# An attention and feed-forward kernel: batch 0 by halves of heads, first units by halves of features, weight columns dealt in pairs

## The chip, the core and the metric

The kernel runs on one core of a Trainium2 chip. The core has five engines with an instruction queue each: TensorE (PE) for matmuls, VectorE (DVE), ScalarE (ACT), GpSimd (POOL) and SyncE (SP), which here only issues DMAs. [...] Engines wait for one another on semaphores. The metric is the device time of one execution in microseconds, the median over runs.

## What is computed

Linear attention, then a feed-forward layer with a gated activation:

```python
q_s = softmax(q, over head_dim)            # q, k, v: 8 batches, 8 heads, 576 rows, 64
k_s = softmax(k, over the rows)
kv  = einsum('bhsd,bhse->bhde', k_s, v)
x   = einsum('bhsd,bhde->bhse', q_s, kv)   # -> 4608 tokens x 512 features
h   = x @ w_in                             # 512 -> 2048
g   = h / (1 + exp(-beta * h))
out = g @ w_out                            # 2048 -> 512
```

## The kernel before

**Tiles.** Every token of x is needed by both dense layers, so x, h and g never leave the chip. Tokens are cut into nine chunks of 512: for each batch the first 512 of its 576 rows (chunks 0 to 6 and 8), and one chunk, the eighth, of the 64 rows left over in each of the eight batches. A chunk passes through 16 units; unit u makes 128 of the 2048 features of h: four matmuls (`h`, over the four 128-wide k tiles of x, L889) into a PSUM bank, a tanh on ACT (`th`, L907), a multiply on DVE (`g`, L924; the sigmoid is written with tanh), and four matmuls with w_out (`o`, L959), one for each 128 tokens, that add into the four accumulators `acc`. After the 16 units the accumulators are copied to SBUF (`oev`) and stored (`st`). Four PSUM banks are a ring (`hT`) for everything else, the other four are `acc`.

**Attention of a batch.** Heads are held two to a tile: j = 0 to 3 counts pairs of heads, J = 0, 1 halves of the heads (J = 0 is j 0 and 1). For q: row maximum (`qmax`, DVE), subtract (`qsub`, POOL), `qexp` (ACT), `qsum` and `qrcp` (DVE), `qnorm` (POOL), transposes (`qtr`, PE, and `qtrev` on ACT or DVE). For k: a maximum over the rows by DVE (`kmax`, then `kred` over the nine row groups, then `kswap` and `ksmall`, which take the larger of partition halves), `krep` spreads it, `ksub` subtracts it (POOL or DVE), `kexp` (ACT). v is cast to bf16 (`vcast`). Then `kv` (72 small matmuls), `kvn` (five DVE instructions that divide by the sum), `x` (eight matmuls), and `xev`, four evictions to xT.

**Order.** All instructions are issued in one order written out by hand, ORDER: each engine runs its own in that order, and waits where an operand isn't there. All loads are issued by SP in that order too. `fill` operations are matmuls with zeros or leftover data that keep PE busy while it waits.

**Batch 0 before.** q's rows come in three parts, h = 0, 1 (four row groups each) and 2 (the ninth). For k the pairs j = 0, 1 are subtracted on PE: `kin` multiplies k by an fp32 identity, `kminus` adds the maximum times minus the identity in the same bank, and `kexp` reads PSUM. `x 0 h J` makes x for half of the tokens, h, from all heads; `h n h x` and `th n h`, `g n h`, `o n h` of units 0 to 3 then run on 256 tokens at a time, two units sharing a bank.

**Weights.** w_in is cut in four blocks of 512 columns, w_out in four of 512 rows, and each of the eight in two halves: 512 KB each, `ld w0` to `ld w7` into four staging buffers, then cast to bf16 (`cast w`). w_in's blocks are w0, w2, w4, w6 and serve units 0-3, 4-7, 8-11, 12-15; their halves are k tiles 0, 1 and 2, 3. w_out's are w1, w3, w5, w7.

**Tail.** For the last eight units the `o` operations are split by token tile, and token tile 3 also by output columns: columns 0-255 stay in acc[3], columns 256-511 go to a ring bank and are copied out by ACT and by DVE, 128 each.

Of the kernel before, what the change touches and what calls it, by code (L numbers as in the profile page):

```python
# [1069 lines left out]
```

## Time and profile before

| | us |
|---|---|
| median of 3 runs (lowest, highest) | 287.24 (287.19, 287.53) |
| the profiled execution | 287.31 |
| its span, first to last instruction | 285.5 |
| PE busy | 275.8 |
| DVE, ACT, POOL busy | 194.9, 174.2, 131.2 |
| DMA moved | 50.01 MB |

The page counts an engine as busy while an instruction of it is under way; matmuls overlap, so the distance between starts says what one costs. The chain of waits is followed back from the last instruction to what released each. In the timelines a row is start, duration, engine, line, operation, result and operands, count, and in brackets the idle time ahead of it with what ended it; rows of the chain are start, duration, what. Rows of groups end with busy time, mean ns of one, and idle time with its releasers. "PEld" is PE's load of a matmul's stationary operand.

### The profile page before, as it was taken

How to read it: one execution, taken by the hardware profiler on the slowest of the kernel's cores; microseconds unless marked ns; L12 is line 12 of the kernel's file. 1: busy time of each engine (PE TensorE's matmuls, PEld its weight loads, DVE VectorE, ACT ScalarE, POOL GpSimd, SP SyncE). 2: the span in 40 equal slices, each digit the busy share in tenths (PEclk: the TensorE clock that was granted, in tenths of full speed). 3: DMA queues.
4: the chain of work that ended last, by engine and by line, in shares of the span. 5: the costliest groups of instructions: out<-in, count | busy, mean ns of one | idle time of the engine just before them, and what ended most of it. 6: DMA issues, size and time to landing. Idle time of an engine off the chain costs nothing.

```text
span 285.5 us, 5163 instructions
## 1 busy us (share of the span) xinstructions
PE 275.8 (97%) x1947; PEld 129.9 (45%) x1977; DVE 194.9 (68%) x394; ACT 174.2 (61%) x291; POOL 131.2 (46%) x93
## 2 busy tenths in 40 slices
PE   7799999999999999999999999999999999999994
PEld 2356544444444544444444544444444444444442
DVE  2998957999899898997667858555754263435421
ACT  2498885887488577837586566564671274345422
POOL 6899996869379948083960650090020000000000
PEclk9999999999999999999999999999999999999999
DMA  7999999990991994991434927000054001005104
GB/s 229 390 391 385 384 389 391 390 336 7 276 371 43 316 275 181 295 329 41 152 119 113 189 62 193 0 3 2 0 141 164 0 0 39 0 0 187 73 0 147
DMA packets 37048, 50.01 MB, mean 175 GB/s; under 512 B 15760, under 2 KB 16160, under 8 KB 37024
## 3 DMA queue, kind: packets, MB, share of 16 engines
q1 hardware_dynamic: 36880, 49.63, 53.4%
q8 instruction: 15, 0.25, 0.3%
q10 hardware_dynamic: 144, 0.07, 0.1%
q14 instruction: 9, 0.07, 0.1%
HBM read 36.71 MB, written 9.44 MB: 162 GB/s over the span
## 4 chain that ended last, share of the span: by engine, by line
PE 91%; DMA 4%; ACT 1%; SPq 1%; issue 1%; DVE 0%
PE hT L889 43%; PE acc L959 42%; DMA kf<-in_k_dram 2%; DMA wst<-in_moe_w_in_dram 2%; PE hT L638 2%; PE hT L688 1%; SPq L275 1%; PE hT L951 1%; PE acc L951 1%; ACT w_in_b L232 0%; PE hT L464 0%; PE hT L734 0%; ACT qT L232 0%; ACT ek L612 0%; ACT ek L605 0%
## 5 line engine op out<-in xcount | busy, mean ns | idle before, releaser
L907 ACT ACTIVATE th<-hT,beta_c 128x512 bf16<-128x512 f32 (+1 forms) x148 | 96.6, 677 | 66.9 <-PE hT L889 48.5
L924 DVE SCALAR_TENSOR_TENSOR g<-th,hT 128x512 bf16<-128x512 bf16 x144 | 94.6, 680 | 58.5 <-ACT th L907 55.5
L959 PE MATMUL acc<-w_out_b,g 128*128 128x512 bf16 x543 | 130.7, 379 | 1.4 <-issue 0.8
L889 PE MATMUL hT<-xT,w_in_b 128*128 128x512 bf16 (+1 forms) x517 | 117.7, 372 | 0.7 <-issue 0.2
L889 PEld LDWEIGHTS <-w_in_b 128*128 128x128 bf16 x592 | 57.6, 98 | 64.8 <-ACT w_in_b L232 0.2
L959 PEld LDWEIGHTS <-g 128*128 128x128 bf16 x560 | 53.7, 98 | 64.5 <-issue 2.9
L560 POOL TENSOR_TENSOR kf<-kf,kmb 128x1152 f32<-128x1152 f32 (+1 forms) x15 | 38.0, 2543 | 23.6 <-DVE kmb L550 17.6
L441 POOL TENSOR_TENSOR qn<-eqe,qz 128x1152 bf16<-128x1152 bf16 (+2 forms) x20 | 34.5, 1739 | 28.0 <-DVE qz L433 18.1
L393 POOL TENSOR_TENSOR qf<-qf,qm 128x1152 f32<-128x1152 f32 (+2 forms) x20 | 34.4, 1733 | 18.4 <-issue 11.9
L378 DVE TENSOR_REDUCE qm<-qf 128x9 f32<-128x576 f32 (+2 forms) x34 | 23.3, 704 | 6.2 <-DMA qf<-in_q_dram 6.2
L422 ACT ACTIVATE eqe<-qf 128x576 bf16<-128x576 f32 (+2 forms) x34 | 21.5, 657 | 9.5 <-POOL qf L393 9.5
L232 ACT CAST xT<-hT 128x512 bf16<-128x512 f32 x19 | 12.6, 740 | 21.1 <-PE hT L688 21.1
L428 DVE TENSOR_REDUCE qs<-eqe 128x9 f32<-128x585 bf16 (+2 forms) x34 | 24.0, 713 | 0.5 <-ACT eqe L422 0.4
L490 DVE TRANSPOSE_TENSOR_REDUCE km<-kf 128x18 f32<-128x576 f32 x32 | 23.6, 754 | 0.0
L612 ACT ACTIVATE ek<-kf 128x576 bf16<-128x576 f32 x30 | 19.5, 683 | 0.9 <-DMA vf<-in_v_dram 0.9
L234 POOL CAST va<-vf 128x1152 bf16<-128x1152 f32 (+1 forms) x11 | 12.0, 1105 | 6.9 <-DMA vf<-in_v_dram 6.9
L889 PE MATMUL hT<-xTt,w_in_b 128*128 128x512 bf16 x63 | 14.9, 379 | 0.1
L234 DVE CAST xT<-hT 128x512 bf16<-128x512 f32 x9 | 6.3, 728 | 7.0 <-PE hT L688 7.0
L232 ACT COPY osb<-acc 128x512 f32<-128x512 f32 x14 | 7.8, 594 | 3.0 <-PE acc L959 3.0
L367 PE MATMUL hT<-g,warm 128*128 128x512 bf16 x21 | 7.0, 482 | 1.6 <-POOL g L240 1.5
L234 DVE COPY osb<-acc 128x512 f32<-128x512 f32 (+1 forms) x6 | 3.8, 632 | 4.9 <-PE acc L951 3.8
L638 PEld LDWEIGHTS <-ek 64*64 64x64 bf16 x576 | 5.7, 106 | 2.2 <-issue 1.3
(74 smaller groups left out, 121.7 us busy)
## 6 DMA issues: line engine op xcount, KB each, us to landing
qf<-in_q_dram SPq DMA_DIRECT2D x14, 576.0 KB, 6.9
kf<-in_k_dram SPq DMA_DIRECT2D x14, 576.0 KB, 7.7
vf<-in_v_dram SPq DMA_DIRECT2D x14, 576.0 KB, 8.4
out_dram<-osb SPq DMA_DIRECT2D x19, 256.0 KB, 2.6
wst<-in_moe_w_in_dram SPq DMA_DIRECT2D x8, 512.0 KB, 7.9
wst<-in_moe_w_out_dram SPq DMA_DIRECT2D x8, 512.0 KB, 11.2
out_dram<-wst SPq DMA_DIRECT2D x16, 256.0 KB, 3.7
qf<-in_q_dram SPq DMA_DIRECT2D x4, 288.0 KB, 4.1
```

The lines of the kernel that those rows point to most:

```text
L234: eng.tensor_copy(dst, src)
L378: dve.tensor_reduce(qm[:, j : j + n, i0:i1], qf[b % 2][:, j : j + n, i0:i1], axis=AX.X, op=ALU.max,)
L393: eng.tensor_tensor(x, x, m, ALU.subtract)
L422: act.activation(eq[:, i0:i1, j : j + n, :].rearrange("p i j d -> p j i d"), x, ACTF.Exp)
L428: dve.tensor_reduce(qs[:, i0:i1, j : j + n].unsqueeze(3), x, axis=AX.X, op=ALU.add)
L441: eng.tensor_tensor(qn[b % 2][:, i0:i1, j : j + n, :], eq[:, i0:i1, j : j + n, :], z, ALU.mult)
L490: dve.tensor_reduce(km[:, j : j + n].rearrange("p j i e -> p (j i e)"), kf[b % 2][:, j : j + n].rearrange("p j i (e c) -> p (j i e) c", c=32),
L560: eng.tensor_tensor(x, x, m, ALU.subtract)
L889: pe.matmul(w, w_in_b[:, kt, u * P : (u + 1) * P], r, start=(kt == 0), stop=(kt == KT - 1),)
L907: act.activation(th[turn(n, h) % 3][:, c], bank(n, h), ACTF.Tanh, scale=beta_c[:, u : u + 1])
L924: dve.scalar_tensor_tensor(out=out, in0=of, scalar=1.0, in1=src, op0=ALU.add, op1=ALU.mult)
L959: pe.matmul(acc[t][:], g[n % NG][:, t * P : (t + 1) * P], w_out_b[:, u, :], start=(u == 0), stop=(u == NJ - 1),)
```

## The change

Batch 0 goes by halves of heads all the way: `kred`, `kswap`, `ksmall`, `kvn` and `x` are done for J = 0 and J = 1 apart, with `krep` and `ksub` for each j (j even on DVE, j odd on POOL); nothing of k is subtracted on PE any more, and the constants for it go. Batch 1's k is treated the same way up to `ksub`. The first two thirds of q of J = 0 are not subtracted by POOL: ACT's exp takes minus the maximum as a bias, one instruction for each row group and j. Units 0 to 3 start with k tiles 0, 1 (the features of J = 0) on all 512 tokens and finish with k tiles 2, 3; units 2 and 3 take two accumulators as their banks (SPARE), so the first `o` waits for their gates.

Unit u makes the columns 256 (u // 2) + 2 c + u % 2 of w_in: two units share 256 neighbouring columns, one the even and one the odd, so the stationary operand of `h` has a step of two. w_out's rows are loaded two neighbouring rows to a partition, and beta is transposed in two strided parts. w_in_b is laid out as block, half, pair of units, and then 512 columns and 64 unused.

The last token tile is cut at column 384 in place of 256: 384 columns in acc[3], 128 in a ring bank, one copy each. ORDER is written anew throughout.

The start of ORDER:

```diff
-ld_q0_0, ld_q0_1, ld_q0_3, consts, qmax_0_2_0, qmax_0_0_0, qmax_0_1_0, qsub_0_2_0=pool, qsub_0_0_0=pool, qexp_0_0_0,
-ld_q0_2, fill_0, ld_k0_3, qmax_0_0_1, ld_k0_1, fill_8, ld_k0_0, qmax_0_1_1, qmax_0_2_1, ld_k0_2, qsub_0_0_1=pool,
...
+consts, ld_q0_1, ld_q0_0, qmax_0_0_j1, qmax_0_0_j0, qmax_0_1_j1, qmax_0_2_0, qexp_0_0_j1, ld_q0_3, qexp_0_0_j0,
+ld_q0_2, qsub_0_2_0=pool, qmax_0_1_j0, qsum_0_0_0, qrcp_0_0_0, qexp_0_2_0, qexp_0_1_j1, qexp_0_1_j0, ld_k0_1,
+qmax_0_1_1, qsub_0_1_1=pool, qmax_0_0_1, qsub_0_0_1=pool, ld_beta, ld_k0_0, ld_v0_0, ld_k0_3, ld_v0_1, kmax_0_1,
+kmax_0_0, qsum_0_1_0, ld_k0_2, ld_v0_2, fill_0, fill_5, fill_7, fill_10, fill_14, ld_v0_3, ld_w0_0, kred_0_0,
+qrcp_0_1_0, qexp_0_1_1, fill_12, fill_6, fill_1, qnorm_0_0_0=pool, fill_3, fill_13, fill_4, kswap_0_0, qtr_0_0_0,
+kmax_0_3, ksmall_0_0, krep_0_1, qexp_0_0_1, qsum_0_0_1, qnorm_0_1_0=pool, ld_w0_1, fill_8, qtrev_0_0_0=act, kmax_0_2,
+qtr_0_1_0, vcast_0_j0=act, fill_2, ksub_0_1=pool, qtrev_0_1_0=act, qrcp_0_0_1, krep_0_0, ld_w2_0, ld_w2_1, kred_0_1,
+ld_q1_1, vcast_0_j1=act, kswap_0_1, qnorm_0_0_1=pool, ksub_0_0=dve, kexp_0_1, ksmall_0_1, fill_11, beta_tr, krep_0_3,
+krep_0_2, kexp_0_0, qtr_0_0_1, ksub_0_3=pool, vcast_0_j3=act, cast_w0_0_1=act, qsum_0_1_1, ksub_0_2=dve, kexp_0_2,
+qrcp_0_1_1, kv_0_0, kexp_0_3, kvn_0_0, ld_w1_0, qmax_0_2_1, qtrev_0_0_1=dve, fill_9, x_0_0, xev_0_0=dve,
+vcast_0_j2=pool, kv_0_1, qnorm_0_1_1=pool, cast_w0_1_0=pool, kvn_0_1, qsub_0_2_1=pool, cast_w0_0_0=pool, qtr_0_1_1,
+xev_0_1=act, h_2_0, h_3_0, cast_w2_0=pool, qtrev_0_1_1=act, ld_w1_1, cast_w2_1=pool, x_0_1, xev_0_3=dve, ld_w4_0,
+cast_w0_1_1=act, qexp_0_2_1, qsum_0_2_0, qsum_0_2_1, qrcp_0_2, qnorm_0_2_1=pool, cast_w1_0=pool, h_0_0, h_1_0,
+ld_w4_1, xev_0_2=act, beta_ev, h_1_1, th_1, ld_q1_0, ld_w3_0, h_0_1, qmax_1_2, h_3_1, h_2_1, ld_k1_1, ld_w6_0,
+qmax_1_3, th_0, g_0, th_2, h_5, g_2, th_5, g_1, th_3, ld_w6_1, g_3, qsub_1_1=pool, h_6, h_4, h_7, th_4, g_5, th_6,
+g_4, g_6, ld_w3_1, cast_w1_1=pool, o_0, o_1, o_2, o_3, qnorm_0_2_0=pool, cast_w4_0=pool, qexp_1_2, qexp_1_3,
...
```

The code:

```diff
-    FILLS = [(14, None)] + [(2, (h, J)) for h in range(2) for J in range(2)] + 8 * [(1, None)]
-    KPE = range(2)
-    QPE = set()
+    FILLS = [(14, None)] + [(2, (h, J)) for h in range(2) for J in range(2)] + 10 * [(1, None)]
+    BIAS = {(0, 0), (1, 0)}
...
-    w_in_b = sbt("w_in_b", [P, KT, FF], BF16)
+    w_in_b = sbt("w_in_b", [P, NJ // 4, 2, 2, 4 * P + 64], BF16)
...
-    w_out_v = w_out.rearrange("(j p) f -> p j f", p=P)
+    w_out_v = w_out.rearrange("(m p r) f -> p m r f", p=P, r=2)
...
-            cast(eng, w_in_b[:, 2 * half : 2 * half + 2, 512 * blk + c0 : 512 * blk + c1], s)
+            m0, m1 = c0 // (2 * P), c1 // (2 * P)
+            dst = w_in_b[:, blk, half, m0:m1, 0 : 4 * P].rearrange("p m (k c) -> p m k c", c=2 * P)
+            cast(eng, dst, s.rearrange("p k (m c) -> p m k c", c=2 * P))
...
-                for c, (c0, c1) in enumerate(((0, P), (P, 512))):
+                for c, (c0, c1) in enumerate(((0, 2 * P), (2 * P, 512))):
...
+    def q_exp_rows(j, n, i0, i1):
+        uses("qmax", *q_parts(0, j, n, i0, i1))
+        made("qexp", *q_parts(0, j, n, i0, i1))
+        made("qsub", *q_parts(0, j, n, i0, i1))
+        for a in range(j, j + n):
+            for i in range(i0, i1):
+                act.activation(eq[:, i, a, :], qf[0][:, a, i, :], ACTF.Exp, bias=qm[:, a, i : i + 1])
...
+    def k_cut(J):
+        return slice(0, KT) if J is None else slice(2 * J, 2 * J + 2)
...
-    def k_swap(b):
-        uses("kred", b)
-        take(("swap", b))
-        made("kswap", b)
+    def k_swap(b, J):
+        uses("kred", *pairs_of(b, 2 * J, 2))
+        take(("swap", b, J))
+        made("kswap", (b, J))
         pe.matmul(
-            place[("swap", b)][:, 0 : 2 * KT],
+            place[("swap", b, J)][:, 0:4],
             swap[:],
-            kmr[:, :, :, 0].rearrange("p j e -> p (j e)"),
+            kmr[:, k_cut(J), :, 0].rearrange("p j e -> p (j e)"),
...
-    def kv_norm(b):
-        uses("kv", (b, 0), (b, 1))
+    def kv_norm(b, J=None):
+        Js = (0, 1) if J is None else (J,)
+        c = slice(Js[0], Js[-1] + 1)
+        uses("kv", *[(b, x) for x in Js])
...
-    def x_mm(b, J, h=None):
-        i0, i1 = (0, NM) if h is None else (4 * h, 4 * h + 4)
+    def x_mm(b, J):
         uses("kvn", (b, J))
...
+            for jp in range(2):
+                place[("x", b, 2 * J + jp)] = acc[2 * jp + J][:]
...
+    SPARE = {2: 0, 3: 2}
+
+    def bank(n):
+        if ("h", n) not in place:
+            if n in SPARE:
+                uses("xT", *[(0, jp) for jp in range(2)])
+                place[("h", n)] = acc[SPARE[n]][:]
+            else:
+                take(("h", n))
+        return place[("h", n)]
...
             pe.matmul(
                 w,
-                w_in_b[:, kt, u * P : (u + 1) * P],
-                r,
+                w_in_b[:, u // 4, kt // 2, u // 2 % 2, 2 * P * (kt % 2) + u % 2 : 2 * P * (kt % 2) + 2 * P : 2],
+                x[:, kt],
...
-    LAST_PIECES = ((0, 0, 256), (1, 0, 128), (1, 128, 128))
+    PIECES = ((0, 384), (384, 512))
...
+            for b in range(2):
+                to = pool if j % 2 else dve
+                op(f"krep {b} {j}", lambda b=b, j=j, to=to: k_rep(b, j, 1, to))
+                op(f"ksub {b} {j}", lambda e, b=b, j=j: k_sub(b, j, 1, e), "pool" if j % 2 else "dve")
...
-        if n < LEAD:
-            for h in range(2):
-                for x in range(2):
-                    op(f"h {n} {h} {x}", lambda n=n, h=h, x=x: st1(n, (x, x + 2), h))
-                op(f"th {n} {h}", lambda n=n, h=h: tanh(n, h))
-                if n % 2 == 0:
-                    op(f"g {n} {h}", lambda n=n, h=h: gate(n, h))
-                op(f"o {n} {h}", lambda n=n, h=h: st2(n, h))
-            continue
-        if n in (16, 17):
+        if n < LEAD or n in (16, 17):
             op(f"h {n} 0", lambda n=n: st1(n, (0, 1)))
             op(f"h {n} 1", lambda n=n: st1(n, (2, 3)))
```

The end of ORDER, after the last `o` operations of token tiles 0 to 2:

```diff
-o_141_3_0, o_142_3_0, o_143_3_0, st_8_1, oev_8_3_0=dve, oev_8_2=act, st_8_2, st_8_3_0, o_140_3_1, o_141_3_1,
-o_142_3_1, o_143_3_1, oev_8_3_1=act, oev_8_3_2=dve, st_8_3_1, st_8_3_2
+oev_8_3_0=act, oev_8_2=dve, st_8_2, o_136_3_1, o_137_3_1, o_138_3_1, o_139_3_1, o_140_3_1, o_141_3_1, st_8_1,
+st_8_3_0, o_142_3_1, o_143_3_1, oev_8_3_1=dve, st_8_3_1
```

The last store is issued on ACT's queue, the one of columns 0-383 on SP's.

More of the change, by code (lines that the diff above doesn't have):

```diff
@@ L359, in fill @@
         done.add(key)
[L360 removed]
+        r, w = g[NG - 1][:], place[key]
         if part is not None:
@@ L928 @@
[L928 to L937 removed]
+        v = NJ // 2 * (u % 2) + u // 2
+        uses("st1", n)
+        if n >= 3:
+            uses("gate", n - 3)
+        made("tanh", n)
+        act.activation(th[n % 3][:], place[("h", n)], ACTF.Tanh, scale=beta_c[:, v : v + 1])
```

523 lines of the change are left out of this document (188 added, 335 removed).

## The prediction

> **What bounds the kernel now.** I read the page first (busy shares, slices, chain), then the chain of waits in order of time, the timelines of TensorE (PE), VectorE (DVE), ScalarE (ACT) and GpSimd (POOL) over the first 40 us, and the groups with shapes kept apart. The page:
>
> ```profile
> PE 275.8 (97%) x1947; PEld 129.9 (45%) x1977; DVE 194.9 (68%) x394; ACT 174.2 (61%) x291; POOL 131.2 (46%) x93
> PE   7799999999999999999999999999999999999994
> PE 91%; DMA 4%; ACT 1%; SPq 1%; issue 1%; DVE 0%
> ```
>
> PE is the bound of every slice but the first two and the last. The chain in order of time (start, us, what) shows where that begins and ends:
>
> ```profile
> 4.03 6.47 DMA kf<-in_k_dram
> 10.52 5.99 DMA wst<-in_moe_w_in_dram
> 16.51 0.67 ACT ek L612
> ...
> 19.72 0.41 PE acc L688 x8
> ...
> 20.67 7.01 PE hT L889 x48
> ...
> 32.11 0.45 PE hT L464 x8
> ...
> 45.10 0.71 PE hT L638 x71
> ...
> 49.16 3.45 PE hT L889 x16
> ...
> 69.89 0.18 PE hT L734 x8
> ...
> 76.86 0.56 PE hT L688 x8
> ...
> 281.44 0.45 PE hT L951 x4
> 281.92 0.28 ACT osb L232
> 282.21 0.29 DVE osb L234
> ```
>
> Until 20.67 us the chain is loads, ACT and small matmuls; from there to 281.9 it is matmuls, 261.2 us. Sixteen of 512 columns take 3.45 us, 215.6 ns each, and the two dense layers are 1152 of them or as many columns: 248.4 us. The seven later batches add kv (0.71) and x (0.56) each, 8.9 us; transposes of batch 1 (0.45 twice) and the tails' eight small products (up to 0.18 each) make some 2. So 259 of the 261.2 us must be done by every version, and the end moves by three things only: when the stream of h matmuls starts, what is added to it or waits in it, and the tail behind it.
>
> **The start.** The twelve loads of batch 0 come in both versions at one pace, all of q before k and v; the new order puts w_in's first block right behind them, where the old one has half of q of batch 1 between. The first h matmuls of the change need features of heads 0 to 3 alone, so k and v of these. By my count DVE is latest there. Its timeline and groups:
>
> ```profile
> 7.63 1.48 DVE L378 TENSOR_REDUCE qm<-qf 128x8 f32<-128x512 f32 x3 [1.68 <-DMA qf<-in_q_dram]
> 9.71 1.26 DVE L428 TENSOR_REDUCE qs<-eqe 128x8 f32<-128x520 bf16 x2
> 11.71 1.39 DVE L490 TRANSPOSE_TENSOR_REDUCE km<-kf 128x18 f32<-128x576 f32 x2
> 18.24 0.23 DVE L657 TENSOR_SCALAR kz<-hT 128x2 f32<-128x2 f32 x2
> 18.72 0.49 DVE L660 TENSOR_TENSOR kvn<-hT,kz 128x128 bf16<-128x128 f32 x2
> ...
> L560 DVE TENSOR_TENSOR kf<-kf,hT 128x576 f32<-128x576 f32 x1 | 0.7, 715 | 0.0
> L433 DVE RECIPROCAL qz<-qs 128x8 f32<-128x8 f32 x4 | 0.5, 168 | 0.0
> L234 DVE CAST xT<-acc 128x512 bf16<-128x512 f32 x2 | 1.4, 740 | 0.2 <-ACT beta_c L349 0.2
> ```
>
> The last of q lands at 7.63. From there the new order gives DVE, ahead of the first kvn: 2 qmax of 128x512 (0.60 apart: 1.2), 4 kmax (half of 1.39: 2.8), 3 qsum (half of 1.26: 1.9), 2 ksub (j 0 and 2 are DVE's now; 0.70: 1.4) and 11 small ones (2 kred, 3 qrcp, 2 ksmall, 4 krep) at some 0.15, near the 168 ns row: 1.65. Sum 8.95: DVE reaches kvn at 16.6. The whole kvn took 18.24 to 19.21, 0.97; half of it is as many instructions on half the columns, I take 0.75: 17.35. x of half 0 on PE is 0.56: 17.9. Its two evictions run side by side on DVE and ACT, 0.74: 18.65, and with the hand-overs **h_2 starts at 18.8**.
>
> The others are not later. Rows of POOL and ACT, groups and timeline:
>
> ```profile
> L393 POOL TENSOR_TENSOR qf<-qf,qm 128x512 f32<-128x512 f32 x4 | 4.1, 1046 | 2.1 <-DVE qm L378 2.1
> L441 POOL TENSOR_TENSOR qn<-eqe,qz 128x512 bf16<-128x512 bf16 x4 | 4.1, 1046 | 0.3
> L560 POOL TENSOR_TENSOR kf<-kf,kmb 128x576 f32<-128x576 f32 x1 | 1.4, 1411 | 0.1
> L422 ACT ACTIVATE eqe<-qf 128x128 bf16<-128x128 f32 x2 | 0.5, 302 | 1.7 <-POOL qf L393 1.7
> ...
> 6.51 0.63 ACT L422 ACTIVATE eqe<-qf 128x512 bf16<-128x512 f32 x1 [4.28 <-POOL qf L393]
> ```
>
> From 8.3 (first qmax of q's second half) POOL has 2 subs and 4 norms of 1.02, 2 ksub of 1.4, a vcast of some 0.65: 9.6, so 17.9, where the last norm is wanted for x of half 1. The sixteen ACT exps with a bias (128x64, an unseen form) take the place of two POOL subs and two large exps. Each costs between nothing and the 302 ns of a 128x128; I take 0.2 for half its columns: 3.2 us, at most 4.8. They need no sub, so they start at about 5, where ACT's first exp now starts at 6.51, and end by 9.8 at the latest, before POOL is through with subtracting q's second half (8.3 + 2 x 1.02 = 10.3). Cost nothing; without that cover it would be the excess over 10.3.
>
> PE then does h_2 and h_3 on two of four k tiles (4 x 0.216), x of half 1 (0.56), h_0 and h_1 while x of half 1 is evicted (0.86 over 0.74), then the other halves: no gap from 18.8. But x of half 1 stands in this stream, and in the old one ahead of it, so 18.8 + 0.56 = 19.4 compares with 20.67: **-1.3 us**. Bounds: 0 if each of DVE's 22 steps costs 0.06 more than I took; -1.9 if the small ones pack 0.1 apart.
>
> **What is added to the stream.** Two kswap of batch 1, fp32, and the strided columns of w_in. Rows of PE's weight loads, and where a cast was late:
>
> ```profile
> 13.42 0.30 PEld L507 LDWEIGHTS hT<-kmr,swap 128*128 128x128 f32 x2
> L889 PEld LDWEIGHTS <-w_in_b 128*128 128x128 bf16 x592 | 57.6, 98 | 64.8 <-ACT w_in_b L232 0.2 <-issue 0.2
> L580 PEld LDWEIGHTS acc<-kf,ident_f 128*128 128x128 f32 x4 | 0.7, 188 | 1.3 <-issue 1.2
> 34.88 1.04 POOL L234 CAST w_in_b<-wst 128x1024 bf16<-128x1024 f32 x1
> 36.38 1.05 ACT L232 CAST w_in_b<-wst 128x1024 bf16<-128x1024 f32 x1
> 37.48 1.08 PEld L889 LDWEIGHTS <-w_in_b 128*128 128x128 bf16 x6 [0.22 <-ACT w_in_b L232]
> ```
>
> A kswap is two passes with two fp32 loads, 0.11 apart: 0.22 each, **+0.4 us**; 0 if loads are pulled under the matmuls ahead, +0.8 if the 0.39 us that the pair spans is exposed.
>
> Strided columns: a load of 128 bf16 two apart covers the 512 bytes per partition that an fp32 load covers, and that one took 188 ns, 0.11 apart. The plain one takes 98 ns and lies under a matmul of 216, so nothing is paid up to there: **0**, and at most 0.1 for each time that PE starts after a wait, some ten times: +1. It is below zero for no reason.
>
> The weights of units 12 on: in the old run PE arrives as ACT's cast ends and loses 0.22. Now PE comes 1.3 earlier. POOL, counted on from the two w_in casts behind its last norm, does qsub 2.1, norms and casts of 1.04 one after another, waits for q's sums of batch 1 until about 29.3 and ends cast_w6_0 at 35.5, 0.4 before the 35.92 of now; ACT's cast behind an exp that waits for POOL ends at some 36.2, PE is there at 35.6 and does half a unit on the first half (0.43): **+0.3 us**; 0 to 1.2 (ACT's cast as late as now).
>
> k of batch 1 by halves puts two ksub (1.4) and two qtrev on DVE. Its waits between 36 and 48 us:
>
> ```profile
> DVE g L924 <- ACT th L907: 3.3, 2, 2.3
> ```
>
> The 3.3 us that it waits for tanh there take them; without that cover they delay gates and come out of the 1.3. The paired rows of w_out halve the number of its packets; the loads of weights are all landed long before PE asks but for those above. Nothing for either.
>
> **The tail.** Before, the last 256 columns are evicted by ACT, then DVE (0.28 and 0.29 in a row, though meant side by side). Now one DVE copy of 128 columns is behind the last matmul: **-0.3 us**; 0 if the 384 columns' store, started 0.5 earlier and three times as large, lands last.
>
> **Sum.** -1.3 + 0.4 + 0.3 - 0.3 = -0.9. The profiled execution took 287.31 us (span 285.5 and 1.8 around it), 0.07 over the median of the runs, 287.24: 287.31 - 0.9 = **286.4 us**.
>
> **The rivals.** (a) *PE's clock falls in the thinner start, slower.* The old start keeps PE busy by fp32 matmuls with the identity, which go away; the fills that stay are ten of 0.22 between 8 and 18.8. The trace shows a slow PE at the very start (windows: sum over 8 to 20 us, then two stretches of the first fills; between them a row of PE's timeline):
>
> ```profile
> sum 12.00, PE 9.96 PEld 5.10 DVE 11.49 ACT 8.72 POOL 11.29; mean PE 1.66 PEld 0.85 DVE 1.91 ACT 1.45 POOL 1.88
> 13.05 0.40 PE L464 MATMUL acc<-ident,qn 128*128 128x128 bf16 x4 [1.08 <-POOL qn L441]
> 1.40:4.90 3.50, 3.45 (x9) 1.00 0.89 254
> 4.90:6.90 2.00, 2.00 (x9) 1.00 0.92 324
> ```
>
> Nine fills take 3.5 us from 1.4 us on and 2.0 after that. From 8 to 20 us PE is now busy 9.96 of 12; of the new 10.8 us I find some 5: 2.2 of fills, 1 of transposes, 1.5 of kv and x. If that lets the slow state return, and it holds as long as at the start, the first 3.5 us of h run 9 where 16 fit: 1.5 us lost, 287.9. It decides once a gap is longer than those that the old run bears, 1.08 us at most; the new one, from the last early fill to the first exp of q's second half, is 8.3 to 10.1 by my count. [...]
>
> (b) *The gain is given back.* POOL, ACT and DVE are near full until 36 us; if ACT's casts are no earlier than now, PE waits 1.2 instead of 0.3 at unit 12: 287.3. For it speaks the 0.22 wait, against it that POOL is rid of two subs of 1.02.
>
> (c) *Waits in the stream go too.* 261.2 less 259 leaves 2.2 us lost inside it; a cast that writes one piece of w_in_b is less tied to matmuls that read its neighbours. Half of it: 285.3. Against it: only 0.2 of PEld's idle time ends on a w_in cast.
>
> (d) *The change of columns does not stay hidden.* If a strided load took four times 98 ns, 392, each of 576 h matmuls would be 176 ns longer: 388. Against it the 188 ns row. [...]
>
> **How the numbers follow.** The forecast 0.46, with 285.7 to 287.1 as its own range; (a) 0.16, (b) 0.16, (c) 0.17, (d) 0.05. The measurement tells 0.2% (0.57 us) from no change. Faster by that is under 286.67: three quarters of the forecast, all of (c), a little of (b): 0.54. Within: the rest of the forecast, most of (b), a little of (a): 0.22. Slower: most of (a), (d), a little of (b): 0.24. The range takes (c) with the start's lower bound and (a) whole: 284.8 to 288.3; (d) is left out.
>
> **What would show it.** First h at 18.8 with x inside the first eight half units; DVE full from 7.6 to 18.6; no PE wait above 0.5 between 19 and 49; first h of chunk 1 at about 48.4 (49.16 now); the strided load under 190 ns and h matmuls 216 apart; one DVE copy behind the last matmul. The prediction is wrong if the h stream starts after 20, if PE waits for ACT or POOL casts above 1 us in all, or if h matmuls stand wider than 216 ns.

## The result and the profile after

The median of 20 runs is 288.78 us (287.24 to 289.88), against 287.21 us of the kernel before (20 runs, 286.51 to 288.28): ratio 1.0043, 95% interval 1.0031 to 1.0056. The change is slower: by 1.6 us between the medians, by 0.9 to 1.6 us by the interval. The forecast was 286.4 with a range up to 288.3, so sign and range were both wrong.

The page of the profiled execution (288.87 us, span 286.8), TensorE's (PE) busy time, its 40 slices, the granted clock in the same slices, and the shares of the chain:

```profile
PE 278.2 (97%) x1950; PEld 127.5 (44%) x1950; DVE 201.3 (70%) x413; ACT 175.5 (61%) x297; POOL 124.6 (43%) x88
PE   7789989999999999999999999999999999999995
PEclk9979999999999999999999999999999999999999
PE 81%; DVE 7%; ACT 6%; DMA 4%; issue 1%; SPq 0%; DVEq 0%; ACTq 0%
```

Two things are new: a 7 in the third slice of the clock, just where the h matmuls begin, and a chain that runs on PE for 10 points less of the span (91% before) and through DVE and ACT instead. PE's timeline shows both places:

```profile
13.65 0.38 PE L358 MATMUL hT<-g,warm 128*128 128x512 bf16 x1
...
14.68 0.40 PE L443 MATMUL acc<-ident,qn 128*128 128x128 bf16 x4 [0.32 <-POOL qn L422]
15.16 0.48 PE L579 MATMUL hT<-va,ek 64*64 64x65 bf16 x36
15.84 0.38 PE L358 MATMUL hT<-g,warm 128*128 128x512 bf16 x1 [0.20 <-DVE kf L548]
16.51 0.77 PE L624 MATMUL acc<-qT,kvn 64*64 64x512 bf16 x4 [0.29 <-DVE kvn L603]
...
18.43 1.77 PE L789 MATMUL acc<-xT,w_in_b 128*128 128x512 bf16 x4
20.13 0.41 PE L624 MATMUL acc<-qT,kvn 64*64 64x512 bf16 x4
...
35.62 0.28 PE L494 MATMUL hT<-kmr,swap 128*128 128x4 f32 x2
36.84 3.00 PE L789 MATMUL hT<-xT,w_in_b 128*128 128x512 bf16 x12 [0.94 <-POOL w_in_b L230]
```

The first h matmul starts at 18.43, as early as forecast (18.8). But four of them take 1.77 us where four take 1.03 or 1.04 elsewhere. And at unit 12 PE stands from 35.62 to 36.84 with nothing but two tiny kswap matmuls, waiting for the weights that POOL casts.

To see where the time lies in every kernel of this study, I cut each trace at three starts of matmuls: the first h matmul, the first h matmul of chunk 1, and the last matmul of all. The h stream of the new order has x of half 1 in it (0.4 us), the old one has it ahead.

| kernel | first h | first h to chunk 1 | chunk 1 to last matmul | span |
|---|---|---|---|---|
| before | 20.57 | 28.43 | 232.60 | 285.5 |
| after | 18.43 | 31.08 | 233.47 | 286.8 |
| e1_fills | 17.67 | 30.34 | 233.26 | 285.0 |
| e2_casts | 18.01 | 30.45 | 233.78 | 286.0 |
| e3_both | 17.90 | 30.86 | 233.26 | 285.8 |
| e4_thin | 21.24 | 28.42 | 232.60 | 286.2 |
| e5_order | 17.83 | 30.04 | 233.25 | 284.9 |
| e6_xfirst | 18.96 | 29.89 | 233.25 | 285.9 |
| e7_tail | 18.22 | 30.80 | 233.25 | 286.1 |
| e8_both | 17.94 | 30.04 | 233.26 | 285.1 |
| e9_gates | 17.76 | 31.27 | 233.25 | 286.1 |
| e10_fewer | 18.92 | 32.17 | 233.64 | 288.5 |
| e11_plain | 18.24 | 30.34 | 233.25 | 285.6 |
| e12_split | 19.68 | 28.42 | 232.99 | 285.0 |

The gain of 2.1 us at the start is gone at chunk 1 (49.00 before, 49.51 after), and another 0.9 is lost behind it. The start itself varies by up to 0.9 us between executions of the same code (20.57 and 19.68 in two kernels that differ only behind 60 us), so single spans are not compared below without their rows, and verdicts are those of the medians.

The other rows that answer to the forecast, of the profile after: the groups of the strided weight loads and of the exps with a bias,

```profile
L789 PEld LDWEIGHTS <-w_in_b 128*128 128x128 bf16 x576 | 56.0, 98 | 68.0 <-issue 1.3
...
L403 ACT ACTIVATE eqe<-qf,qm 128x64 bf16<-128x64 f32 x16 | 4.1, 335 | 2.1 <-DVE qm L369 2.1
```

POOL's timeline ahead of unit 12,

```profile
30.62 2.12 POOL L422 TENSOR_TENSOR qn<-eqe,qz 128x1152 bf16<-128x1152 bf16 x1 [2.51 <-DVE qz L414]
32.70 1.04 POOL L230 CAST w_out_b<-wst 128x1024 bf16<-128x1024 f32 x1
33.69 2.12 POOL L385 TENSOR_TENSOR qf<-qf,qm 128x1152 f32<-128x1152 f32 x1
35.75 1.04 POOL L230 CAST w_in_b<-wst 128x1024 bf16<-128x1024 f32 x1
```

and the end of the timeline of all engines:

```profile
282.60 0.61 PE L845 MATMUL hT<-w_out_b,g 128*128 128x128 bf16 x8
282.80 0.48 ACT L228 COPY osb<-acc 128x384 f32<-128x384 f32 x1 [0.23 <-PE acc L845]
283.25 0.29 DVE L230 COPY osb<-hT 128x128 f32<-128x128 f32 x1 [1.86 <-PE hT L845]
283.57 0.67 ACTq L887 DMA_DIRECT2D out_dram<-osb  x1
```

A strided load takes 98 ns, as the plain one did. POOL idles 2.5 us for the sums of batch 1 and then does a norm, a cast and a subtraction before it comes to unit 12's weights (the last row). At the end one copy of 0.29 stands behind the last matmul, as forecast, and yet from the end of that copy (283.54) to the end of the span (286.76) are 3.22 us, where there were 3.02 before.

### The profile page after: what moved, and what is told of

It reads as the page before. It is cut to its first block, busy times and chain, and to the rows that moved or that the text cites. A ratio compares the mean times of both kernels' runs of the same rounds, so it can differ in the third digit from the quotient of the medians.

```text
span 286.8 us, 5150 instructions
## 1 busy us (share of the span) xinstructions
PE 278.2 (97%) x1950; PEld 127.5 (44%) x1950; DVE 201.3 (70%) x413; ACT 175.5 (61%) x297; POOL 124.6 (43%) x88
## 2 busy tenths in 40 slices
DMA packets 35864, 50.01 MB, mean 174 GB/s; under 512 B 15736, under 2 KB 16000, under 8 KB 35840
## 4 chain that ended last, share of the span: by engine, by line
PE 81%; DVE 7%; ACT 6%; DMA 4%; issue 1%; SPq 0%; DVEq 0%; ACTq 0%
PE acc L853 38%; PE hT L789 37%; DMA kf<-in_k_dram 3%; ACT th L806 2%; DVE g L814 2%; PE hT L579 2%; DVE km L469 1%; DMA qf<-in_q_dram 1%; PE hT L624 1%; DVE qs L409 1%; ACT ek L555 1%; DVE qm L369 1%; PE acc L845 1%; ACT xT L228 1%; ACT wst L228 1%
## 5 line engine op out<-in xcount | busy, mean ns | idle before, releaser
L806 ACT ACTIVATE th<-hT,beta_c 128x512 bf16<-128x512 f32 x142 | 93.9, 689 | 68.1 <-PE hT L789 41.9
L853 PE MATMUL acc<-w_out_b,g 128*128 128x512 bf16 x560 | 134.2, 380 | 0.0
L789 PE MATMUL hT<-xT,w_in_b 128*128 128x512 bf16 x504 | 118.2, 379 | 1.1 <-POOL w_in_b L230 0.9
L385 POOL TENSOR_TENSOR qf<-qf,qm 128x1152 f32<-128x1152 f32 (+2 forms) x18 | 32.4, 1814 | 7.6 <-DVE qm L369 7.6
L369 DVE TENSOR_REDUCE qm<-qf 128x9 f32<-128x576 f32 (+3 forms) x36 | 23.4, 671 | 4.5 <-DMA qf<-in_q_dram 4.5
L555 ACT ACTIVATE ek<-kf 128x576 bf16<-128x576 f32 x32 | 21.3, 684 | 0.1
L230 POOL CAST va<-vf 128x1152 bf16<-128x1152 f32 (+1 forms) x8 | 8.7, 1088 | 18.7 <-DMA vf<-in_v_dram 18.7
L228 ACT CAST va<-vf 128x1152 bf16<-128x1152 f32 (+1 forms) x10 | 10.2, 1018 | 0.1
L228 ACT COPY osb<-acc 128x512 f32<-128x512 f32 (+1 forms) x11 | 6.0, 588 | 6.5 <-PE acc L853 6.3
L230 DVE COPY osb<-acc 128x512 f32<-128x512 f32 x9 | 6.0, 685 | 3.2 <-PE acc L853 3.1
```

Of the source, the lines that this page charges most:

```text
L228: act.copy(dst, src)
L369: dve.tensor_reduce(qm[:, j : j + n, i0:i1], qf[b % 2][:, j : j + n, i0:i1], axis=AX.X, op=ALU.max, negate=minus,)
L385: eng.tensor_tensor(x, x, m, ALU.subtract)
L555: act.activation(ek[b % 2][:, j : j + n], kf[b % 2][:, j : j + n], ACTF.Exp)
L789: pe.matmul(w, w_in_b[:, u // 4, kt // 2, u // 2 % 2, 2 * P * (kt % 2) + u % 2 : 2 * P * (kt % 2) + 2 * P : 2], x[:, kt], start=(kt == 0), ...
L806: act.activation(th[n % 3][:], place[("h", n)], ACTF.Tanh, scale=beta_c[:, v : v + 1])
```

## The experiments

**The theory and its rival.** Theory A: the loss is the half clock at the start. Rival B: it is POOL, ACT and DVE between 25 and 45 us, which give back what the start gains. Four kernels, on one chip, against a kernel before of 287.01 us (30 runs).

### e1_fills: PE kept busy

```diff
-    FILLS = [(14, None)] + [(2, (h, J)) for h in range(2) for J in range(2)] + 10 * [(1, None)]
+    FILLS = [(14, None)] + [(2, (h, J)) for h in range(2) for J in range(2)] + [(n, None) for n in (1, 1, 1, 3, 3, 1, 4, 1, 1, 1)]
```

> The changed kernel with seven more fill matmuls of 512 columns (1.5 us of PE) between 11.5 and 16.5 us. Theory 1, the clock fell because PE had too little to do in one window before the first h: granted clock back to 0.999 or 1.000, the four first h matmuls 0.216 apart in place of 0.427, time 287.6 to 288.0 (288.8 less 0.8 to 1.2). Rival: the lost time at the start is covered by the wait for the casts of unit 12, which do not depend on PE: clock 1.0, but the wait at 36 us grows by as much and the time stays at 288.8. Second rival: the clock falls for another reason, clock stays at 0.993.

Measured: 287.83 us (11 runs), ratio to before 1.0029 (1.0017 to 1.0041). The median is 0.95 below that of the changed kernel, and 0.75 when each is set against its own kernel before. The record of the clock goes in steps of 3.41 us. The windows view of the profile after, cut at these steps (length, busy time and count of PE, PEld, DVE, ACT, POOL; then the granted clock, 0.50 for half):

```profile
9.69:13.10 3.41, 2.36 (x15) 1.01 (x14) 3.38 (x11) 2.20 (x5) 3.41 (x4) 1.00 1.05 393
13.10:16.52 3.42, 2.25 (x49) 1.33 (x48) 3.32 (x16) 3.42 (x7) 3.42 (x4) 1.00 1.05 390
16.52:19.93 3.41, 3.29 (x48) 1.79 (x48) 2.08 (x9) 2.82 (x6) 3.41 (x6) 0.50 1.06 401
```

and of e1_fills, cut at the steps of its own record:

```profile
11.87:15.29 3.42, 3.14 (x55) 1.78 (x54) 3.39 (x11) 3.42 (x8) 3.42 (x4) 1.00 1.03 376
15.29:18.70 3.41, 3.00 (x67) 1.56 (x55) 2.89 (x15) 3.13 (x7) 3.41 (x7) 1.00 1.07 403
```

The kernel before has a window with as little PE work as that of the profile after, in 16 matmuls in place of 49, and keeps the clock:

```profile
12.02:15.43 3.41, 2.23 (x16) 1.38 (x17) 3.34 (x9) 3.36 (x9) 3.36 (x4) 1.00 1.04 383
```

After the change PE runs at half clock from 16.52 to 19.93, through x, kv and the first h matmuls. With seven more fills it doesn't. The mean clock of each run says the same without a profile: 18 of the changed kernel's 20 runs have 0.995 or less, and all 11 of e1_fills 0.998 or more. The fills make half clock rare, not impossible: of the 73 runs of the seven other kernels below that have the same fills, 11 are at 0.994, and they are 0.4 to 1.9 us (1.0 on the mean) slower than the other runs of their kernel. So theory A holds for some 1 us by the medians; by the ratios, whose intervals overlap, for only 0.4. A loss of 0.8 us (0.5 to 1.2) is left with a full clock. In it is the wait of rival B:

```profile
34.12 0.28 PE L494 MATMUL hT<-kmr,swap 128*128 128x4 f32 x2
35.34 3.00 PE L789 MATMUL hT<-xT,w_in_b 128*128 128x512 bf16 x12 [0.94 <-POOL w_in_b L230]
```

PE comes to unit 12 1.5 us earlier than in the profile after and waits the same 1.2 us. POOL's row shows why: the norm that started at 30.62 starts 1.5 us earlier as well.

```profile
29.12 2.13 POOL L422 TENSOR_TENSOR qn<-eqe,qz 128x1152 bf16<-128x1152 bf16 x1 [2.13 <-DVE qz L414]
```

### e4_thin: the old start made thin

The kernel before without the 16 fills behind the first 14: `(2, (h, J))` and `(1, None)` in its FILLS become `(0, (h, J))` and `(0, None)`.

> The kernel before without its sixteen fills after the first fourteen (nothing of the output depends on them). Theory 1: PE's clock falls in it too, granted clock 0.994 or less, and the time rises by 0.8 to 1.7 us to 288.0 to 289.0. Rival: the fp32 products with the identity keep PE busy enough, or the clock does not depend on fills: 0.999, and the time stays at 287.2.

Measured: 286.98 us (12 runs), ratio 1.0011 (0.9996 to 1.0026). The clock falls here too: 10 of 12 runs are at 0.994 or less, against 0.998 and more for the kernel before, and the profile has half clock from 15.10 to 18.52. The time doesn't rise as theory 1 expected: the median is that of the kernel before (287.01). The nine runs at 0.994 have a mean of 287.30, against 286.71 of the two at 1.0 and 286.90 of the kernel before's 30 runs: 0.4 to 0.6 us, less than these runs scatter. That the clock follows what PE does, and not the change's code as such, is shown. The price is smaller than in the new start, where the h matmuls lie in the stretch.

### e10_fewer: the new start made thinner still

The opposite of e1_fills: the changed kernel with `(0, (h, J))` and `10 * [(0, None)]`.

> The changed kernel without the 18 fill matmuls behind the first 14, the opposite of the run with seven more. Theory A (the clock is halved after a stretch in which PE streams too little): the slow stretch comes in every run and starts earlier or comes twice, the mean clock falls to 0.98 to 0.99, and the time is 0.3 to 1.5 above the change's 288.78. Theory B (the slow clock of the change has another cause than what PE does between 8 and 18 us): clock and time are those of the change, 288.78 within 0.3.

Measured: 289.14 us (6 runs), ratio to its own before (287.07, 15 runs) 1.0086 (1.0067 to 1.0106); mean clock 0.976 to 0.982 in every run. Its windows:

```profile
9.19:12.60 3.41, 1.05 (x7) 0.82 (x7) 3.38 (x9) 1.64 (x3) 3.41 (x5) 0.50 1.05 389
12.60:16.02 3.42, 2.49 (x40) 1.85 (x44) 3.38 (x11) 3.42 (x7) 3.40 (x3) 0.50 1.04 389
16.02:19.43 3.41, 2.63 (x74) 1.70 (x63) 2.91 (x15) 2.82 (x6) 3.41 (x7) 0.50 1.06 396
19.43:22.84 3.41, 3.41 (x12) 0.94 (x11) 1.26 (x6) 1.81 (x5) 1.96 (x2) 0.50 1.02 383
```

Four stretches of 3.41 us at half clock instead of one. Seven fills more, none, 18 fewer give 287.83, 288.78 and 289.14 (ratios 1.0029, 1.0043 and 1.0086): theory A, in the order of the doses.

### e2_casts and e3_both: the casts of unit 12 earlier

ORDER of the changed kernel, alone (e2) and with e1's fills (e3):

```diff
-... cast_w3_0=pool, ... qsub_1_0=pool, ... cast_w6_0=pool, o_4, o_5, ... qexp_1_0, cast_w6_1=act
+... cast_w3_0=pool, ... cast_w6_0=pool, qsub_1_0=pool, ... o_4, o_5, ... cast_w6_1=act, qexp_1_0
```

> The changed kernel with the casts of the last quarter of w_in put one place earlier on their engines: POOL's ahead of the subtraction of q 1 of J = 0, ACT's ahead of the exp that waits for that subtraction. Theory 2, PE waits 1.4 us at unit 12 (1.19 and 0.23) for these two casts alone: the wait goes, the time falls by 1.0 to 1.4 us to 287.4 to 287.8, slow clock unchanged. Rival: POOL is the bound up to 49 us, so the subtraction that is now 1 us later makes kv or x of batch 1 late by as much, and the time stays within 0.4 us of 288.8.

> Both edits at once. If theory 1 and theory 2 are the two causes and add up: 288.8 less 2.2 = 286.4 (286.1 to 286.8), faster than the kernel before by 0.6 to 1.0 us. If one covers the other: 287.3 or more.

Measured: 288.14 (9 runs; 1.0046, 1.0029 to 1.0063) and 288.13 (11 runs; 1.0046, 1.0031 to 1.0062). PE's timeline of e2_casts:

```profile
35.19 2.81 PE L789 MATMUL hT<-xT,w_in_b 128*128 128x512 bf16 x12 [0.45 <-DVE g L814]
...
41.11 0.39 PE L494 MATMUL hT<-kmr,swap 128*128 128x4 f32 x2 [0.32 <-DVE kmr L488]
```

The wait at unit 12 is shorter and has another releaser, DVE's gate, and a new one stands at kswap_1_0. That matmul starts 23.10 us behind the first h, as in e1_fills: PE now comes to it earlier, and the maximum that DVE makes for it is ready no earlier. (This profile has a full clock; the other eight runs of e2 have 0.994 or less.) e2's median is 0.6 below the changed kernel's, but its ratio to before is no lower (1.0046 against 1.0043), so no gain is shown. With the fills, e3 is no better than e1 alone, and the two edits don't add up. Moving these two casts by themselves only moves the wait.

### e5_order: POOL's idle time used as well

In e1's profile the load of w_out's block 1 lands at 28.5 us (issue at 20.71 and 7.8 to landing), while POOL idles until 29.12 for qz. So cast_w3_0 goes ahead of that norm, with the fills and the casts of e3. A second set of four, against a kernel before of 286.98 us (33 runs).

```diff
-... qnorm_1_1=pool, ... cast_w3_0=pool, ...
+... cast_w3_0=pool, qnorm_1_1=pool, ...
```

> The changed kernel with the seven more fills and three casts moved: cast_w3_0 ahead of qnorm_1_1 on POOL (which sits idle 2.1 us there, until qz of 29.1 us), cast_w6_0 ahead of qsub_1_0 on POOL, cast_w6_1 ahead of qexp_1_0 on ACT. With the fills alone the profile has the loads of unit 12's two halves landing at 31.5 and 32.9 us and their casts starting at 34.25 and 34.93. Theory A (the start's gain is lost because POOL and ACT stand in another order than the data): the casts start at about 31.6 and 33.4, PE's waits of 1.19 and 0.23 us go down to under 0.2, and 1 us or so reaches the end: 286.7 to 287.0. Theory B (the engines are simply full up to chunk 1, so any order gives the wait back): new waits of the k chain of batch 1 appear between 37 and 45 us, and the time stays at 287.6 to 288.1, as with the fills alone (287.83).

Measured: 287.45 us (12 runs), ratio 1.0014 (0.9996 to 1.0032). Two timelines of its profile, POOL's

```profile
28.77 1.04 POOL L230 CAST w_out_b<-wst 128x1024 bf16<-128x1024 f32 x1 [1.36 <-DMA wst<-in_moe_w_out_dram]
...
31.84 1.04 POOL L230 CAST w_in_b<-wst 128x1024 bf16<-128x1024 f32 x1
```

and PE's:

```profile
35.02 2.81 PE L789 MATMUL hT<-xT,w_in_b 128*128 128x512 bf16 x12 [0.45 <-DVE g L814]
...
40.52 0.39 PE L494 MATMUL hT<-kmr,swap 128*128 128x4 f32 x2
```

The cast of unit 12 starts at 31.84 instead of 34.25. PE gains 0.3 us up to chunk 1 (30.04 against 30.34 in the table) of the 1.2 that the wait was worth: now it is DVE's gate that frees the PSUM bank (the 128x512 fp32 that h's matmuls write, `hT`) for h_13. The median goes down by 0.38, with intervals that overlap, and e5's takes in 1, no difference from the kernel before. Two of the 12 runs, at a clock of 0.994, took 289.3. Between the two expectations: another order gives back a part of the wait, and the next engine in line holds the rest.

### e9_gates: the next wait taken on

On top of e5_order, DVE does g_11 and g_10 ahead of kmax_1_3 and kred_1_1, h_13 goes ahead of kswap_1_1, and cast_w3_1 ahead of ksub_1_3:

```diff
-... h_11, kmax_1_3, kred_1_1, ... g_11, ... g_10, o_4, o_5, kswap_1_1, ksmall_1_1, cast_w6_1=act, ... ksub_1_3=pool, ... h_13, ... cast_w3_1=pool
+... h_11, ... g_11, ... g_10, kmax_1_3, kred_1_1, qtrev_1_1=dve, o_4, o_5, cast_w6_1=act, h_13, kswap_1_1, ksmall_1_1, ... cast_w3_1=pool, ksub_1_3=pool
```

> The fills and the casts as moved before, and the next wait taken on: with the casts early enough PE waits 0.49 us at 34.3 us for DVE, which has g of unit 10 (it frees h_13's PSUM bank) behind two kmax and a kred. Here DVE does g_11 and g_10 ahead of kmax_1_3 and kred_1_1, kswap_1_1 stands behind h_13, and POOL does cast_w3_1 ahead of ksub_1_3. Theory A (what is left at unit 12 is order alone): PE starts h_13 at about 34.3 to 34.5, its waits between 33 and 42 us go from 1.06 in all to 0.5 or less, and the time is 286.7 to 287.2, no slower than before. Theory B (DVE, POOL and ACT are full until chunk 1, each order pays elsewhere): the k chain of batch 1 is late and PE waits for w_out's cast, kswap_1_0 or kv, and the time stays at 287.4 to 287.9.

Measured: 287.92 us (7 runs; before 287.07), ratio 1.0040 (1.0025 to 1.0055). PE's timeline:

```profile
33.20 0.62 PE L443 MATMUL hT<-ident,qn 128*128 128x128 bf16 x8 [0.55 <-POOL qn L422]
...
39.39 1.02 PE L789 MATMUL hT<-xT,w_in_b 128*128 128x512 bf16 x4 [0.26 <-DVE kf L548]
...
41.68 0.39 PE L494 MATMUL hT<-kmr,swap 128*128 128x4 f32 x2 [0.40 <-DVE kmr L488]
```

h_13 no longer waits for the gate, and three other waits, on POOL, DVE and DVE, add up to as much. (The first is in part a w_out load that landed 1.2 us later in this execution than in e5's.) Theory B holds for this order too. That no order would do isn't shown: three others than the one as written were tried.

### e6_xfirst: the halves of features undone

With e1's fills, h_2_0 and h_3_0 behind x of half 1 and its evictions:

```diff
-... xev_0_1=act, h_2_0, h_3_0, ... x_0_1, xev_0_3=dve, ... h_0_0, h_1_0, ld_w4_1, xev_0_2=act
+... xev_0_1=act, ... x_0_1, xev_0_3=dve, ... xev_0_2=act, h_2_0, h_3_0, h_0_0, h_1_0, ld_w4_1
```

> The changed kernel with the seven more fills, and the first units by halves of features undone: h_2 and h_3 on features 0 and 1 no longer stand ahead of x of the second half, all h matmuls wait for both. The h stream then starts some 0.8 to 1.0 us later (18.5 to 19.3 against 17.67 plus the 0.56 of x). Theory A (the wait at unit 12 swallows whatever the start gains): the stall at 34 us shrinks by as much, 1.2 to about 0.3, and the time stays within 0.3 of 287.83. Theory B (the start's gain reaches the end, and the loss is elsewhere): the stall stays near 1.2 and the time is 288.5 to 288.9.

Measured: 288.13 us (10 runs), ratio 1.0039 (1.0025 to 1.0052), 0.3 above e1 with overlapping intervals. PE's timeline:

```profile
18.96 1.04 PE L789 MATMUL acc<-xT,w_in_b 128*128 128x512 bf16 x4
...
36.19 3.00 PE L789 MATMUL hT<-xT,w_in_b 128*128 128x512 bf16 x12 [0.95 <-POOL w_in_b L230]
```

I had expected the wait at unit 12 to shrink by what the start lost, if it is what swallows the start's gain. It doesn't: the start is later by 0.85 us (18.96 against 17.67 plus the 0.44 of x), and the wait is 0.95 on POOL as before. So it isn't a fixed time that PE arrives at too early. POOL's norm waits for the sums, these for exps that ACT does between tanhs of the units before: the wait follows the h stream. The norm starts 5.00 us ahead of PE's arrival at unit 12 in all three profiles (30.62 and 35.62 after, 29.12 and 34.12 in e1, 29.96 and 34.96 here). In the profiles the later start is kept up to chunk 1 (48.85 here, 48.01 in e1). In the medians it isn't clear of noise, and 288.13 lies where theory A had it, though theory A's smaller wait didn't come.

### e7_tail and e8_both: the last store on the other queue

With e1's fills, `act if x else sp` becomes `sp if x else act` in the last two stores; e8_both adds the order of e5.

> The changed kernel with the seven more fills, and the queues of the last two stores exchanged: the last 128 columns leave on SP's queue, the 384 ahead of them on ACT's. In the profiles the last copy on DVE ends 3.26 us ahead of the span's end after the change and 3.0 before it, the issue on ACT takes 0.67 us and on SP 0.54, and the time outside the span is 2.1 after and 1.8 before. Theory A (issuing the last store on ACT costs the tail's gain): 0.15 to 0.5 us faster than 287.83, 287.3 to 287.7, with the copy 3.0 from the end. Theory B (the tail is what a store takes, on any queue): 287.83 within 0.15, still some 3.2 from the end.

> The fills, the three casts moved and the two queues exchanged together. If the casts' order and the queue are what is left of the loss, this gives 286.3 to 286.8, below the kernel before (287.0). If both theories B hold, 287.6 to 288.1.

Measured: 287.81 us (12 runs; 1.0023, 1.0010 to 1.0035) and 287.58 us (12 runs; 1.0025, 1.0007 to 1.0043). The end of e7's timeline:

```profile
282.53 0.29 DVE L230 COPY osb<-hT 128x128 f32<-128x128 f32 x1 [1.86 <-PE hT L845]
282.59 0.66 ACTq L887 DMA_DIRECT2D out_dram<-osb  x1
```

The copy ends 3.33 us from the end of the span (286.15), against 3.22 with ACT's queue. The time outside the span is 1.94 on the mean of e7's runs and 2.12 of e1's, so that the queue is worth some 0.1 us in all, which the medians don't show. The queue is at most a part of what the tail's gain was lost to. No version of the new order beats the kernel before; only e5_order can't be told from it.

### e11_plain: the columns not dealt

With e1's fills, unit u takes 128 neighbouring columns; w_out's rows and beta are ordered to match.

```diff
-                w_in_b[:, u // 4, kt // 2, u // 2 % 2, 2 * P * (kt % 2) + u % 2 : 2 * P * (kt % 2) + 2 * P : 2],
+                w_in_b[:, u // 4, kt // 2, u // 2 % 2, 2 * P * (kt % 2) + P * (u % 2) : 2 * P * (kt % 2) + P * (u % 2) + P],
...
-    w_out_v = w_out.rearrange("(m p r) f -> p m r f", p=P, r=2)
+    w_out_v = w_out.rearrange("(m r p) f -> p m r f", p=P, r=2)
```

> The changed kernel with the seven more fills, and the dealing of columns undone: unit u takes 128 neighbouring columns of w_in, w_out's rows and beta are ordered to match (a transfer of w_out then reads two rows of 2 KB in place of one piece of 4 KB). Theory A (a strided load costs PE nothing, as the 98 ns of its row say): 287.83 within 0.3. Theory B (the pairs cost something at each start behind a wait, or their larger packets bring weights sooner): at least 0.4 off, faster by the first, slower by the second.

Measured: 287.93 us (9 runs; before 287.07), ratio 1.0032 (1.0018 to 1.0045), against 1.0029 of e1; the load takes 98 ns here too. Neither the stride nor the larger packets of w_out (35864 packets in all on the page of the profile after, 36888 on this one's) make a difference beyond the 0.3 us of theory A.

### e12_split: the stream broken twice more

This one is on the kernel before. The table's fourth column is 232.60 in both profiles of the old order and 233.25 or 233.26 in eight of the eleven of the new one, to a hundredth: not a matter of chance, and far behind the start. (The other three, after, e2 and e10, have one more wait of 0.2 to 0.5 us each, near 97 to 99 us.) The new ORDER lists all batches anew, and the small matmuls of kv and of the last token rows (xt) stand in other places. One group in the profile before, xt with kv right behind it,

```profile
69.82 0.25 PE L734 MATMUL hT<-qT,kvn 64*64 64x64 bf16 x8
69.90 0.81 PE L638 MATMUL hT<-va,ek 64*64 64x65 bf16 x72
```

and in the profile after xt by itself, with o matmuls right behind it:

```profile
69.58 0.26 PE L659 MATMUL hT<-qT,kvn 64*64 64x64 bf16 x8
69.76 1.04 PE L853 MATMUL acc<-w_out_b,g 128*128 128x512 bf16 x4
```

By the starts in the traces, the first small matmul of a group follows the big one ahead by 309 ns instead of 216, and a big one follows the last small one of kv or xt by some 125 (in seven of the nine groups of the profile after, three of the eight before) instead of some 10: 0.09 + 0.12 = 0.21 us for such a group. Behind 50 us the old order has 13 groups, the new one 15.

```diff
-... o_22, o_23, ... xt_0, ... kv_2_0, kv_2_1
+... o_22, xt_0, o_23, ... kv_2_0, kv_2_1
...
-... kv_6_0, kv_6_1, kvn_6, xt_5, xtev_5_1=dve, xtev_5_0=dve, o_91
+... kv_6_0, kv_6_1, kvn_6, o_91, xt_5, xtev_5_1=dve, xtev_5_0=dve
```

> The kernel before with one thing of the new order alone: two groups of small matmuls in the stream behind chunk 1 cut in two (xt_0 stands one o unit ahead of kv_2, at about 69.8 us, xt_5 one o unit behind kv_6, at 191.2 us), so the big stream is broken 15 times instead of 13, as in the changed kernel. From the first h matmul of chunk 1 to the start of the last matmul all profiles of the changed order so far but three take 233.25 us, and both of the old order 232.60. Theory A (each break costs about 0.21 us, 0.09 at its start and 0.12 at its end, which was not in the forecast): the segment takes 233.0, and the median is 0.2 to 0.6 above before's. Theory B (the breaks are free, the 0.65 has another cause): 232.6, and no change of the median beyond 0.2.

Measured: 287.68 us (12 runs; before 287.11, 17 runs), ratio 1.0023 (1.0007 to 1.0039), and 232.99 in the trace. PE's timeline has the group cut in two:

```profile
68.05 0.25 PE L734 MATMUL hT<-qT,kvn 64*64 64x64 bf16 x8
68.24 1.04 PE L959 MATMUL acc<-w_out_b,g 128*128 128x512 bf16 x4
69.20 0.78 PE L638 MATMUL hT<-va,ek 64*64 64x65 bf16 x72
```

The fourth column grows by 0.39 for two breaks, where 0.42 were worked out. Theory A: 0.4 of the 0.65 are the two breaks; the other 0.25 are not accounted for.

## Why the prediction was wrong

By its own steps:

- **The start, -1.3: right, and small for what came.** DVE was ahead of the forecast (x of half 0 starts at 16.51, forecast 17.35), the first h stood at 18.43 (forecast 18.8), and with a full clock at 17.67 to 18.24. e6's profile keeps the difference in start up to chunk 1; that it reaches the end isn't clear of noise in the medians.
- **Rival (a), the clock: this is the step that failed first.** It was put at 0.16 and its price at 1.5 us, and the sum took the clock at nothing. The low chance took a gap of 1.8 us, longer than the 1.08 that the old run bears, to leave the clock alone, which no run had shown. The half clock came in 18 of 20 runs and cost some 1 us (0.95 between the medians of after and e1). The wrong part of the argument is the point from which it decides, a single long gap. The gap from 8.3 to 10.1 didn't come: the longest in the profile after between 8.3 and 16.5 is 0.43 us. In the window ahead of the half clock none is above 0.32; PE was at work for 2.25 of 3.42 us, in 49 matmuls, most of them small. e7's profile has a gap of 0.91 in a window that kept the clock. Half clock comes in stretches of 3.41 us (one in the profile after, four in e10), and PE was busy for 2.25 us of the window ahead of them in the profile after, 2.01 in e4's and 0.97 in e10's.
- **Added to the stream, +0.4 and +0.3: together half of what came.** From the first h to chunk 1 the new order takes 30.34 us with a full clock (e1), of which 0.44 is x, and the old one 28.43: 1.5 us against a forecast of 0.7. The two kswaps cost some 0.1 each by the starts in the trace. The term that was mis-sized is the casts at unit 12: 1.19 and 0.23 us between starts, in e1 as in the profile after, instead of 0.3. POOL's work was sized right, 6.2 us from its wait for q's sums (29.3) to the end of the cast (35.5), and 6.17 in both profiles. What failed is the other path: the forecast had PE at unit 12 6.3 us behind the end of POOL's wait (35.6), and PE comes 5.0 behind it, at 34.12 in e1, where the wait ends at 29.12, and at 35.62 in the profile after, where it ends at 30.62. The sums follow the h stream, so an earlier start brings both forward and leaves the wait. The upper bound, 1.2, was set for ACT's cast; that POOL's gave the same is luck.
- **Rival (b), the gain given back there: happened too.** It stood with a chance of 0.16 and 287.3, the clock with 0.16 and 287.9. I treated the two as alternatives, and they came together. By the forecast's own prices that is 286.4 + 1.5 + 0.9 = 288.8; that it meets the measured time is luck, for the clock cost less, and two terms below are not in it.
- **"The end moves by three things only": failed.** The 259 us "done by every version" leave out where the small matmuls break the stream. The new order breaks it twice more behind chunk 1. It loses 0.65 us there, of which e12 shows 0.4 to be the breaks.
- **The tail, -0.3: the copy as forecast, the gain not.** From the start of the last matmul to the end of the last copy are 0.90 us before and 0.55 after. The store behind it takes 2.0 us from issue to landing before, and 2.2 after. The bound that the forecast named didn't happen: the store of 384 columns lands at 285.55, the one of 128 last, at 285.74. A further 0.33 us lies outside the span (1.78 before, 2.11 after, on the mean of the runs), of which e7 puts 0.2 down to the queue. Together the tail is 0.2 longer, where 0.3 less was forecast; why a store and the end outside the span take longer stays open.
- **Strided columns, 0: right**, in the row (98 ns with a step of two, 98 without) and in e11 (no difference beyond 0.3 us). The forecast leaned on the 188 ns of an fp32 load, below the 216 of a matmul; the load took half of that.
- **Sixteen exps at 0.2 each, hidden: right.** Four of them follow one another in 1.07 us, and the last ends at 8.65, ahead of the 9.8 of the forecast. A single one takes 335 ns, more than the 302 that were its upper bound; their starts are 0.24 apart.

The sum, with what the runs showed: start -1.7 (first h at 18.0 on the mean of the nine profiles with the new start, plus 0.44 for x, against 20.1 on the mean of before and e12), waits and kswaps +1.5, behind chunk 1 +0.65, tail and outside the span +0.2: +0.6 with a full clock, where e1 has +0.8 (0.5 to 1.2). The clock adds some 1 us. The measured 1.6 is that sum within what the start varies.

What stays open: 0.25 us of the stream behind chunk 1, the longer last store and time outside the span, and the part of batch 1's k by halves alone, whose undoing needs an order of its own and wasn't tried.

## What to carry to other kernels

When a change makes a stretch thinner, count what PE streams in every 3.41 us of it (the step of the clock's record here), not its longest gap (0.32 us in the window ahead of the half clock after the change), and price the clock in the forecast itself. A gain at the start of a long stream is only kept if the engines that feed the next stretch have slack: add up their work to the point where PE meets them, with what each instruction waits for, and treat two mechanisms that don't exclude each other as a sum. And where an order is written anew, compare the whole of it: here two groups of small matmuls more, far behind the part that was meant to change, cost 0.4 us.

## What the hardware showed that was not expected

- The clock was halved behind a window without a gap above 0.32 us. Counted by columns (512 in 216 ns), PE streamed full bf16 matmuls (128*128 in the rows) for 0.65 us in the window 13.10 to 16.52 of the profile after, and small ones (64*64) besides; the next window ran at half clock. In e2_casts' profile a window with 1.08 us kept it. Where between them the clock turns, and what the small ones count for, no run here settles. The busy share doesn't tell: a window of 2.10 us busy kept the clock in e7, and 2.25 lost it here.
- The windows lie differently against the program in each execution: the first step that the record of a profile has lies at 4.82 to 7.34 us. Of the changed kernel's 20 runs, 2 had a mean clock of 1.0 (287.5 us on the mean), 3 of 0.992 (287.65), 7 of 0.993 to 0.994 (288.9), 7 of 0.987 to 0.988 (288.9) and one of 0.982 (289.6). A lower clock doesn't cost the same each time.
- A group of small matmuls (kv or xt) between big ones costs some 0.2 us beyond its own work: 0.39 for two in e12. The distance at its start is 308 to 310 ns in every group behind 50 us of the profiles before and after. At its end it is 124 to 127 in ten of the 17 groups of kv or xt, and 145 to 534 in the other seven.
- From the end of the last copy to the end of the span are 3.0 to 3.3 us, whichever queue issues the last store: 2.0 to 2.3 from its issue to its landing, and 1.0 behind that.
